# Channel mixing by quarters: seven products in place of eight, on one core

## Chip, cores, metric

One Trainium2 chip (trn2), one of its cores. The metric is the device time of the whole kernel in microseconds (us).

## The reference, cut to what matters

Attention with normalised queries and keys, then an MLP mixer on its output. Everything is fp32 except the four mixer weights, which arrive as 64-bit floats.

```python
# q, k, v: (8, 12, 448, 64)
scores = scale * rmsnorm(q, g_q) @ rmsnorm(k, g_k).transpose(0, 1, 3, 2)
x = softmax(scores) @ v            # then (B, H, S, D) -> (B, S, H*D) = (8, 448, 768)
h = relu(x^T @ w_tok1) @ w_tok2    # token mixing:   448 -> 256 -> 448
u = x + h^T
h2 = relu(u @ w_ch1) @ w_ch2       # channel mixing: 768 -> 1536 -> 768
return u + h2
```

Channel mixing is the larger part: per batch 2 x 72 products of 128x128 weights with 448 columns.

## The kernel before

The eight batches form a pipeline: while TensorE does the MLP of batch b, the attention of batch b+1 is merged between its products. All weights stay in SBUF as fp32. They are made from 64-bit words in 80 chunks of 128x256 (72 for the channel layers), at the start: some beside batch 0's attention, the rest beside batch 0's MLP.

```python
def convert_first(i):     # VectorE: exponent and mantissa bits of the high word
    nc.vector.tensor_scalar(e, hi, 0x7FF00000, None, ALU.bitwise_and)
    nc.vector.tensor_scalar(m, hi, 0x000FFFFF, None, ALU.bitwise_and)
def convert_second(i):    # ScalarE: both as floats
    nc.scalar.activation(out=e, in_=e, func=AF.Relu, bias=expo_c, scale=8.0)
    nc.scalar.activation(out=mf, in_=m, func=AF.Identity, bias=one_c, scale=2.0**-20)
def convert_last(i):      # VectorE: low word and sign; GpSimd: the product
    nc.vector.scalar_tensor_tensor(out=mf, in0=lo, scalar=2.0**-52, in1=mf, op0=ALU.mult, op1=ALU.add)
    nc.vector.scalar_tensor_tensor(out=e, in0=hi, scalar=0x80000000, in1=e,
                                   op0=ALU.bitwise_and, op1=ALU.bitwise_or)
    nc.gpsimd.tensor_tensor(out=dst, in0=fold(mf), in1=fold(ef), op=ALU.mult)

def weight_items(lo, hi):
    def one(i):           # one weight step: three chunks in flight, a load two ahead
        ... convert_first(i); convert_second(i - 1); convert_last(i - 2); weight_load(i + 2)

def ch1(b, f, part):      # 6 products of 448 columns, relu by ScalarE
    for cc in range(part * half, part * half + half):
        nc.tensor.matmul(out=ps[:, 0:S], lhsT=wc1_sb[:, cc, f * P:(f + 1) * P],
                         rhs=st["uT", b][:, cc, :], start=(cc == 0), stop=(cc == NC - 1))
    if part == 1:
        nc.scalar.activation(out=st["h2"][:, f, :], in_=ps[:, 0:S], func=AF.Relu)

def ch2(b, cc, part):     # 12 products of 448 columns, added to u by VectorE
    ...
# order: merge() interleaves lists by their estimated cost
early = merge(early, weight_items(BEFORE, len(chunks) + 2))     # batch 0 only
for _, fn in merge(att, early + late): fn()
```

The order in which `merge` emits the instructions is their order in each engine's queue, so it sets what stands behind what (the stretch from 241 us below shows VectorE standing 4.6 us at one instruction with others behind it).

## Time and profile before

| | before |
|---|---|
| time, median (4 runs) | 1544.6 us (1543.6 to 1547.2) |
| TensorE busy | 1489.2 us, 96% |
| batch 0's MLP | 84 to 288 us |
| a full later batch | 186.7 us |

The start times come from the first transpose of each batch's MLP. In all lines of the profile PE is TensorE's products, PEld its weight loads, DVE VectorE, ACT ScalarE, POOL GpSimd, and SPq the SyncE queue that issues the loads and stores; L181 is line 181 of that run's kernel.

### The profile page before, as it was taken

What the parts mean: (1) busy time and instruction counts of PE and PEld (TensorE: products, weight loads), DVE (VectorE), ACT (ScalarE), POOL (GpSimd) and SP (SyncE); (2) the same over time, 40 slices, a digit from 0 to 9 for tenths busy, and PEclk for the clock granted to TensorE, in tenths of its full rate; (3) what the DMA queues carried; (4) which work ended last, traced back from release to release, by engine and by line L of the source; (5) the groups of instructions that cost most, each with busy time, mean ns of one, the idle gap of its engine ahead of it and who ended that gap; (6) DMA issues with size and microseconds to landing.
All of it is one profiled execution on the core that took longest, in us unless ns stands there. A gap on an engine that the chain in (4) does not pass through costs nothing.

```text
span 1543.7 us, 13746 instructions
## 1 busy us (share of the span) xinstructions
PE 1489.2 (96%) x5248; PEld 715.6 (46%) x5248; DVE 470.8 (30%) x831; ACT 489.9 (32%) x890; POOL 369.7 (24%) x234
## 2 busy tenths in 40 slices
PE   5879999999999999999999999999999999999998
PEld 2334444544444444454445444444444444445554
DVE  5977777231222212231222221223112222112000
ACT  5855655322223232233222323222322323111100
POOL 6755555121212113111221122112211212000000
PEclk9999999999999999999999999999999999999999
DMA  5434443101011010111001100020001100000001
GB/s 122 127 95 120 123 134 113 36 19 30 24 36 37 18 30 24 36 36 30 24 18 36 48 24 18 19 66 24 18 18 36 54 18 7 7 19 18 0 6 31
DMA packets 121742, 65.73 MB, mean 43 GB/s; under 512 B 91780, under 2 KB 111748, under 8 KB 121668
## 3 DMA queue, kind: packets, MB, share of 16 engines
q1 hardware_dynamic: 111138, 53.53, 13.4%
q10 hardware_dynamic: 10530, 11.24, 2.5%
q8 instruction: 43, 0.70, 0.2%
q14 instruction: 31, 0.25, 0.0%
HBM read 53.74 MB, written 11.01 MB: 42 GB/s over the span
## 4 chain that ended last, share of the span: by engine, by line
PE 88%; DVE 4%; DMA 2%; ACT 2%; POOL 1%; issue 1%; SPq 0%; ACTq 0%; DVEq 0%; POOLq 0%
PE m_ps L417 28%; PE m_ps L430 26%; PE s_ps L236 10%; PE o_ps L293 9%; PE m_ps L393 5%; PE m_ps L401 4%; PE m_ps L307 2%; PE t_ps L221 2%; PE t_ps L374 2%; DMA raw<-in_moe_w_ch_dram 1%; POOL rs L572 1%; ACT qkT L223 1%; DVE e_t L148 1%; DVE m_t L149 1%; DVE es L283 1%
## 5 line engine op out<-in xcount | busy, mean ns | idle before, releaser
L430 PE MATMUL m_ps<-h,wc_sb 128*128 128x448 f32 x1152 | 450.4, 542 | 1.5 <-DVE dt L319 1.5
L417 PE MATMUL m_ps<-uT,wc_sb 128*128 128x448 f32 x1152 | 447.8, 543 | 0.0
L417 PEld LDWEIGHTS m_ps<-uT,wc_sb 128*128 128x128 f32 x1152 | 214.3, 190 | 215.7 <-issue 204.9
L430 PEld LDWEIGHTS m_ps<-h,wc_sb 128*128 128x128 f32 x1152 | 212.6, 190 | 207.5 <-issue 206.1
L242 ACT ACTIVATE e<-s_ps,rs 112x448 f32<-112x448 f32 x384 | 212.2, 635 | 185.6 <-PE s_ps L236 184.0
L279 POOL TENSOR_TENSOR es<-e 112x896 f32<-112x896 f32 x48 | 100.1, 2085 | 677.2 <-PE m_ps L307 564.3
L572 POOL TENSOR_TENSOR rs<-ms,mhalf_c 112x16 f32<-112x16 f32 (+1 forms) x49 | 146.0, 2981 | 219.7 <-DVE ms L571 219.0
L236 PE MATMUL s_ps<-qkT 64*112 64x448 f32 x768 | 171.7, 567 | 9.4 <-ACT qkT L223 9.4
L293 PE MATMUL o_ps<-e,vt 112*64 112x448 f32 x768 | 165.5, 552 | 0.0
L421 ACT ACTIVATE h<-m_ps 128x448 f32<-128x448 f32 x96 | 52.2, 544 | 351.0 <-PE m_ps L417 351.0
L319 DVE STREAM_TRANSPOSE dt<-m_ps 128x448 f32<-128x448 f32 x48 | 31.2, 650 | 403.7 <-PE m_ps L307 403.6
L283 DVE TENSOR_TENSOR es<-es,e 112x896 f32<-112x896 f32 x96 | 112.5, 1172 | 76.4 <-ACT e L242 71.7
L435 DVE TENSOR_TENSOR uT<-uT,m_ps 128x448 f32<-128x448 f32 x48 | 29.8, 620 | 330.5 <-PE m_ps L430 330.4
L223 ACT ACTIVATE qkT<-t_ps,g_t 128x448 f32<-128x448 f32 x96 | 58.8, 632 | 206.6 <-PE t_ps L221 206.3
L236 PEld LDWEIGHTS s_ps<-qkT 64*112 64x112 f32 x768 | 62.1, 174 | 107.6 <-issue 87.6
L393 PE MATMUL m_ps<-x,w_sb 112*128 112x384 f32 x256 | 91.1, 506 | 19.4 <-ACT x L379 11.2
L293 PEld LDWEIGHTS o_ps<-e,vt 112*64 112x64 f32 x768 | 46.6, 136 | 108.8 <-issue 108.8
L567 DVE TENSOR_REDUCE ms<-sq 112x16 f32<-112x1024 f32 (+1 forms) x49 | 58.5, 1195 | 117.4 <-ACT sq L564 117.4
L181 POOL TENSOR_TENSOR wc_sb<-m_t,e_t 128x256 f32<-128x256 f32 x72 | 61.8, 866 | 87.0 <-DVE e_t L179 85.4
L401 PE MATMUL m_ps<-w_sb,h 128*128 128x448 f32 x192 | 78.1, 552 | 2.5 <-DVE uT L406 2.5
L379 ACT COPY y<-t_ps 112x512 f32<-112x512 f32 x48 | 28.0, 585 | 156.6 <-PE t_ps L374 156.6
L393 PEld LDWEIGHTS m_ps<-x,w_sb 112*128 112x128 f32 x256 | 47.8, 194 | 57.0 <-ACT x L379 16.6
(43 smaller groups left out, 775.2 us busy)
## 6 DMA issues: line engine op xcount, KB each, us to landing
raw<-in_moe_w_ch_dram SPq DMA_DIRECT2D x72, 256.0 KB, 2.7
vt<-in_v_dram SPq DMA_DIRECT2D x48, 224.0 KB, 2.6
qk<-in_q_dram SPq DMA_DIRECT2D x92, 112.0 KB, 2.8
qk<-in_k_dram SPq DMA_DIRECT2D x92, 112.0 KB, 3.0
out_dram<-y ACTq DMA_DIRECT2D x14, 672.0 KB, 4.4
out_dram<-y ACTq DMA_DIRECT2D x6, 224.0 KB, 2.9
raw<-in_moe_w_tok_dram SPq DMA_DIRECT2D x4, 224.0 KB, 4.6
raw<-in_moe_w_tok_dram SPq DMA_DIRECT2D x2, 256.0 KB, 2.8
```

The costliest lines, as they stand in the source:

```text
L181: nc.gpsimd.tensor_tensor(out=dst, in0=fold(mf), in1=fold(ef), op=ALU.mult)
L223: nc.scalar.mul(st["qkT", p][:, i, :], ps[:, 0:S], g_t[:, i:i + 1])
L236: nc.tensor.matmul(out=ps[0:R, 0:S], lhsT=qkT[a * D:(a + 1) * D, 1, kc * R:(kc + 1) * R], rhs=qkT[a * D:(a + 1) * D, 0, :], start=True, st ...
L242: nc.scalar.activation(out=e[0:R, a, i, :], in_=pss[a][0:R, 0:S], func=AF.Exp, scale=st["rs", p][0:R, r:r + 1])
L279: nc.gpsimd.tensor_tensor(out=es[0:R], in0=e[0:R, :, 0, :], in1=e[0:R, :, 1, :], op=ALU.add)
L283: nc.vector.tensor_tensor(out=es[0:R], in0=es[0:R], in1=e[0:R, :, i, :], op=ALU.add)
L293: nc.tensor.matmul(out=o[a * D:(a + 1) * D, 0:S], lhsT=vt[0:R, a, kc * D:(kc + 1) * D], rhs=e[0:R, a, i, :], start=(kc == 0), stop=(kc == ...
L393: nc.tensor.matmul(out=ps[:, 0:HC], lhsT=w1_sb[0:R, c, jc * P:(jc + 1) * P], rhs=st["x", h][0:R, c, :], start=(c == 0), stop=(c == NS - 1))
L401: nc.tensor.matmul(out=ps[:, 0:S], lhsT=st["h1", jc][:, cc * P:(cc + 1) * P], rhs=w2_sb[:, jc].rearrange("p c r -> p (c r)"), start=(jc == ...
L417: nc.tensor.matmul(out=ps[:, 0:S], lhsT=wc1_sb[:, cc, f * P:(f + 1) * P], rhs=st["uT", b][:, cc, :], start=(cc == 0), stop=(cc == NC - 1))
L430: nc.tensor.matmul(out=ps[:, 0:S], lhsT=wc2_sb[:, f, cc * P:(cc + 1) * P], rhs=st["h2"][:, f, :], start=(f == 0), stop=(f == NF - 1))
L572: nc.gpsimd.tensor_tensor(out=rs[0:R, w], in0=ms[0:R, w], in1=self.mhalf_c[0:R].to_broadcast([R, (hi - lo) * n]), op=ALU.pow)
```

## The change

Both channel layers are cut into quarters (half of the contraction by half of the outputs; the 448 columns into two times 224), and each 2x2 block product is done with seven products in place of eight, in the form that needs few sums (Winograd's form of Strassen's). This needs four sums or differences of the weights' quarters, four of the moving quarters, and a chain of sums of the products. The intent: 1/8 of the channel arithmetic off TensorE. The eight weight blocks (four quarters, four sums) don't fit into SBUF, so they are written to a DRAM buffer once, and each batch streams them back in 42 units of 384 KB, with seven unit buffers.

```diff
-    wc1_sb = const.tile([P, NC, DC], F32, name="wc1_sb")
+    ws1 = dram.tile([KF // 2, NQ, P, KC, 2, P], F32, name="ws1")      # ws2, ws3 likewise
-    ps_O = pool("ps_O", 2, space=PSUM)
-    ps_M = pool("ps_M", 2, space=PSUM)
+    ps_O = pool("ps_O", 1, space=PSUM)
+    ps_M = pool("ps_M", 3, space=PSUM)
...
+    def combine(j):               # after each pair of chunks
+        w, group, m, t = stages[j]
+        q = st.pop("stage")
+        nc.vector.tensor_tensor(out=q[:, 4], in0=q[:, 1], in1=q[:, 3], op=ALU.add)
+        nc.vector.tensor_tensor(out=q[:, 6], in0=q[:, 1], in1=q[:, 0], op=ALU.subtract)
+        nc.gpsimd.tensor_tensor(out=q[:, 5], in0=q[:, 4], in1=q[:, 0], op=ALU.subtract)
+        nc.gpsimd.tensor_tensor(out=q[:, 7], in0=q[:, 2], in1=q[:, 5], op=ALU.subtract)
...
+        nc.sync.dma_start(out=to.rearrange("q p n -> p q n"), in_=q[:])
...
+        at = i - len(first)       # at the end of convert_last(i)
+        if at >= 0 and at % 2 == 1:
+            combine(at // 2)
...
+    PRODUCTS = ((0, "B11"), (2, "B21"), (5, "T2"), (6, "T3"), (4, "T1"), (7, "B22"), (3, "T4"))
...
+    def ch1(b, mp, i):            # product i of 7: 2 x 3 matmuls of 224 columns
+        for j in range(2):
+            for t in range(KC):
+                nc.tensor.matmul(out=ps[:, j * HS:(j + 1) * HS], lhsT=w[:, t, j, :], rhs=m,
+                                 start=(t == 0), stop=(t == KC - 1))
...
+        elif i == 4:              # the sums of products, some by GpSimd
+            nc.scalar.copy(out=r[5], in_=got)
+            add(nc.gpsimd, h("B22"), r[5], r[3])
+            add(nc.gpsimd, r[2], r[2], r[5])
+        elif i == 5:
+            add(nc.vector, r[1], got, r[2])
...
-            early = merge(early, weight_items(BEFORE, len(chunks) + 2))
+            then = len(first) + 2 * stage_end[3] + 2
+            early = merge(early, weight_items(BEFORE, then))
+            late = merge(late[:14], weight_items(then, len(chunks) + 2)) + late[14:]
```

Cuts are marked by "...". Attention and token mixing are as before, but for the accumulators above and the output tiles.

## The prediction

> **What bounds the kernel now.** I read the page first: the busy row, the slices and the chain of the end.
>
> ```profile
> PE 1489.2 (96%) x5248; PEld 715.6 (46%) x5248; DVE 470.8 (30%) x831; ACT 489.9 (32%) x890; POOL 369.7 (24%) x234
> ...
> PE   5879999999999999999999999999999999999998
> ...
> DVE  5977777231222212231222221223112222112000
> ...
> POOL 6755555121212113111221122112211212000000
> ...
> L430 PE MATMUL m_ps<-h,wc_sb 128*128 128x448 f32 x1152 | 450.4, 542 | 1.5 <-DVE dt L319 1.5
> L417 PE MATMUL m_ps<-uT,wc_sb 128*128 128x448 f32 x1152 | 447.8, 543 | 0.0
> ```
>
> TensorE is the bound in nearly all of the span, and the two channel products (L417, L430) are 898 of its 1489 us. The other engines are a quarter to a third busy on the mean, but not at the start: in the first seven slices (270 us) VectorE shows 5 to 9 tenths and GpSimd 5 to 7. That is where the weights are converted from 64-bit words (80 chunks, the last at 268 us). So there are two stages, and I read them apart, in the table of busy times by stretch (PE, PEld, DVE, ACT, POOL):
>
> ```profile
> 20.00:84.00 64.00, 55.65 (x290) 21.82 (x288) 57.18 (x103) 54.57 (x104) 52.00 (x34) 1.00 0.45 113
> 84.00:130.00 46.00, 35.23 (x124) 17.68 (x122) 33.01 (x73) 21.53 (x46) 23.78 (x19) 0.90 0.37 103
> 130.00:270.00 140.00, 136.53 (x464) 63.33 (x464) 101.60 (x255) 80.57 (x168) 75.04 (x67) 1.00 0.43 121
> 507.00:694.00 187.00, 185.39 (x659) 89.03 (x658) 44.95 (x64) 52.89 (x91) 37.01 (x18) 1.00 0.12 30
> ```
>
> The last row is one steady batch: 1.6 us of idle TensorE in 187. Before 84 us (attention of batch 0 alone, with the first weights) VectorE is 89% busy. Batch 0's MLP runs from 84 to 288 us, where the next batch's first transpose starts (from the start times of the transposes in the trace). Each later full batch takes 186.7 us (start times 474.8, 661.5, 848.2).
>
> How fast is a matmul? Weight loads in the timeline, where nothing else stands between:
>
> ```profile
> 801.13 0.19 PEld L430 LDWEIGHTS m_ps<-h,wc_sb 128*128 128x128 f32 x1 [0.19 <-issue]
> 801.50 0.19 PEld L430 LDWEIGHTS m_ps<-h,wc_sb 128*128 128x128 f32 x1 [0.19 <-issue]
> ```
>
> Every fp32 product is two instructions, and one starts each 0.3755 us for 448 columns.
>
> And why are VectorE's 30 to 70% dear at the start? Two rows:
>
> ```profile
> 109.06 2.13 POOL L279 TENSOR_TENSOR es<-e 112x896 f32<-112x896 f32 x1
> ...
> 109.18 2.17 DVE L149 TENSOR_SCALAR m_t<-raw 128x256 uint32<-128x256 uint32 x1
> ```
>
> A VectorE instruction that usually takes 0.28 us stood for 2.17, until GpSimd's was over.
>
> **What the Trainium skill says.** (1) "TensorE: Matmul & The Clock Gate", section "Back-to-back issue gap": columns / 2.4 + 2.5 ns, but in a stream of load-and-multiply pairs 81 ns at 128 columns where the formula has 56. The trace agrees with the formula at 448 columns taken twice per column (2 x 448 / 2.4 + 2.5 = 375.8); for the transposes' 128 columns it has 109 ns, again 2 x 128 / 2.4 + 2.5, so no penalty for loads there. (2) "SBUF — State Buffer", section "Who interferes with whom": a VectorE instruction with two SBUF inputs, or in a 2-port mode, and a GpSimd one that reads SBUF exclude one another for the whole instruction. The two rows above agree; during GpSimd's pow (2.9 us at 113.5) VectorE's weight work ran on at its usual 0.28 to 0.42 us, so pow doesn't do it here. (3) "DMA: Bandwidth & Descriptors", section "Anatomy of one DMA": about 2.0 us plus bytes at 436 GB/s (fitted there to another issuing path). A 256 KB weight chunk lands in 2.7 us here; the formula has 2.6.
>
> **The change, part by part.**
>
> *Removed on TensorE.* Per batch the two channel layers are 2 x 72 products of 448 columns: 288 instructions x 0.3758 = 108.2 us. Now each is 7 quarter products: 3 x 7 x 2 x 3 = 126 in the first, 7 x (2 + 1) x 6 = 126 in the second, of 224 columns: 504 instructions x (2 x 224 / 2.4 + 2.5 = 189.2 ns, an estimate) = 95.3 us. **Gain 12.9 us a batch, 103 us in all**; the 1/8 less arithmetic loses 0.6 us to the fixed 2.5 ns. A 128-column weight load is shown at 190 ns, starting with the matmul before it; but a transpose starts 24 ns before its load's shown end, so the load just hides. This is the closest call.
>
> *Added, steady batches.* VectorE: per 448-column pass 0.62 us (L435's row): 21 in layer 1 (13 us), 14 in layer 2 (half of them 224 wide, 7 us), six small differences (2 us), less the 6 old adds (3.7): 45 becomes 64 us. GpSimd: twelve 448-wide at about 1.1 us (from 2085 ns for 896), four more and ten of 224: 37 becomes 65. ScalarE: 53 becomes 61. In a batch of 174 us none is near a bound. The chain product 4 - ScalarE copy - two GpSimd adds - VectorE add takes some 3.8 us against 2.3 us of one product, and three accumulators give two products of slack; a GpSimd burst (sum, pow, scale: 7 us a head pair) can use that up now and then. I choose **+1.5 us a batch, 10 us in all**.
>
> *Moved to DMA.* 42 units of 393 KB a batch, 132 MB in all, 16.5 MB in 174 us or 95 GB/s, where the start already moves 121. A unit lands in about 2.9 us (estimate by point 3), and it is asked for six units, some 13 us, ahead. Hidden after batch 0.
>
> *Added, batch 0.* Here is the price. The 72 big chunks are converted as before, and each pair of chunks gets two VectorE and two GpSimd sums of 128x128 (about 0.2 and 0.42 us, scaled from 0.34 and 0.73 for 256) and a store. Both layers' sums must be out and back before use. I count the time in which VectorE or GpSimd (pow left out) has an instruction open, since they mostly exclude each other: in the trace 60.6 of the 64 us up to 84, and 127 of 140 from 130 to 270. A steady batch has 50, of which 41 attention; so the 54 chunks from 130 to 270 cost (127 - 0.685 x 41 - 5) / 54 = 1.74 us each.
> - Stage 1 takes 23 weight steps in place of 16: 7 x 1.74 + 6 sums x 1.24 = 20 us: ends at 104 in place of 84.
> - Batch 0's token mixing and layer 1 carry 47 chunks: 82 us, their sums 29, 65% of a batch's attention 27, the MLP's own VectorE work 21 and the part of its GpSimd work that can't overlap, some 12: 171 us, against TensorE's 70 + 34 = 104. **So VectorE and GpSimd become the bound of this stage**; at 98% use it ends near 278. I choose 275 (some PSUM reads overlap).
> - The first unit of layer 2 waits for the last store and its own load: two DMAs of about 3 us and GpSimd's work, 8 us.
> - Layer 2, 12 weight steps beside it in its first part: 48; again a store and a load, 4 visible; the last third 25.
> Batch 0 ends at 275 + 8 + 48 + 4 + 25 = 360; before, 288: **72 us lost**, 59 of it if I allow for a better overlap than in the stretches measured. I choose 63.
>
> Sum: 1545 - 7 x 12.9 (batches 1 to 7) + 10 + 63 = 1528; batch 0's gain is inside its 63. I shade to **1525 us**.
>
> **The rivals.** (a) The preparation is hidden after all: from 130 to 270 us TensorE was 97% busy beside it, so there may be more room than the open-instruction count shows (a blocked instruction counts as open). Then batch 0 loses 20 us and the time is about 1485. (b) Half-width products don't run at 189 ns: if the load shows by 11 ns, 504 x 8 x 0.011 = 44 us more, about 1570. For it: the skill's 81 ns; against: 109 ns in the transposes. (c) The in-order queues bite in steady batches: ScalarE's relu waits for GpSimd, the exps stand behind it. At 5 us a batch: 1550. (d) The unit loads bind: 95 GB/s against up to 216 seen for moments at the start speaks against it.
>
> **Range and chances.** 1485 to 1560: rival (a) is the low end, (b) or (c) in part the high end. Faster by 2% means under 1514.4: batch 0 has to lose 52 us or less with the steady gain whole, 38%. Slower by 2% (over 1576) needs (b) or (c) in full with my batch 0: 4%. The rest, 58%, is within 2%.
>
> **What would show it.** The quarter products' weight loads 0.189 us apart; later batches about 175 us long; VectorE and GpSimd at 8 to 9 tenths up to some 270 us, and TensorE at 6 to 7 tenths there; a gap of 6 to 10 us before layer 2 of batch 0, ended by a DMA; the second batch's first transpose at about 350. Wrong if that transpose starts before 320 (preparation cheaper) or a batch takes over 180 (products or queues dearer).

## More of the kernel before

The prediction shows the main lines of the page. Here are three more: the granted TensorE clock in tenths over 40 slices of the span, the share of the DMA engines' time, and the loads of the weight chunks (count, size, us to landing).

```profile
PEclk9999999999999999999999999999999999999999
DMA  5434443101011010111001100020001100000001
...
raw<-in_moe_w_ch_dram SPq DMA_DIRECT2D x72, 256.0 KB, 2.7
```

The clock is at 90% or more in every slice, the DMA engines are half busy while the weights come in and nearly idle after. So TensorE is the bound, and a change that takes arithmetic from it seems right.

## The result

The kernel after takes 1571.3 us (median of 4, 1569.4 to 1573.3), before 1544.6: the ratio is **1.017** (95% interval 1.0151 to 1.0189). A ratio is the mean time of one kernel's fast runs over that of the other's of the same rounds, so not quite the ratio of the medians. The change made the kernel slower by 1.7%: inside 2%, but outside the range of 1485 to 1560. Results are correct.

The page of the kernel after: busy row, five rows of slices (tenths in 40 slices of the span), and the group of one channel layer.

```profile
PE 1422.2 (90%) x6976; PEld 1054.9 (67%) x6976; DVE 662.5 (42%) x1183; ACT 511.1 (33%) x930; POOL 612.6 (39%) x514
...
PE   5765866497999999999999999999999999999997
...
DVE  5765866743344233432434234433343225322321
...
POOL 5674566644235324333235224352334234320231
PEclk9786997798999999999999999999999999999999
DMA  5456667476244552455244542555254433444353
...
L581 PE MATMUL m_ps<-hb,unit 128*128 128x224 f32 x2016 | 402.0, 357 | 31.4 <-DMA unit<-ws 31.4
```

TensorE has 67 us less of busy time, and the span is 28 us longer. From the 11th slice on it is full as before. In the first ten slices (393 us) it is at 4 to 9 tenths, its clock is no longer full, and yet VectorE shows only 3 to 8 tenths and GpSimd 4 to 7. The table by stretch has the columns of the prediction (busy us and count of PE, PEld, DVE, ACT, POOL, then clock, DMA share, GB/s). The stretches are batch 0's attention, its token mixing, its layer 1, its layer 2, and one steady batch:

```profile
20.00:112.00 92.00, 67.58 (x283) 24.85 (x280) 68.28 (x136) 58.66 (x113) 62.38 (x50) 0.85 0.45 122
112.00:185.00 73.00, 45.85 (x151) 21.57 (x150) 47.26 (x112) 28.66 (x60) 39.52 (x45) 0.77 0.61 179
185.00:292.00 107.00, 80.87 (x361) 60.58 (x360) 75.51 (x177) 46.90 (x96) 65.03 (x71) 0.87 0.68 205
292.00:400.00 108.00, 73.07 (x367) 59.63 (x366) 53.56 (x114) 30.55 (x61) 49.56 (x55) 0.84 0.63 191
574.90:749.40 174.50, 172.41 (x875) 129.50 (x874) 65.33 (x98) 55.27 (x97) 63.04 (x44) 1.00 0.44 127
```

The last row is the steady gain as predicted: a batch takes 174.5 us, before 186.7. So the two traces differ in two ways:

| | before | predicted | after |
|---|---|---|---|
| attention of batch 0 ends | 84 | 104 | 112.5 |
| batch 0's layer 1 ends | | 275 | 292 |
| batch 0's layer 2 really starts | | 283 | 318 |
| batch 1's MLP starts | 288 | 360 (63 lost, so 351, in the sum) | 400 |
| from there to the end | 1255.5 | 1175 | 1171 |

From batch 1 on the kernel gains 84 us; up to there it loses 112.

### The profile page after: what moved, and what is told of

Same layout as the page of the kernel before. It is cut to its first block, busy times and chain, and to the rows that moved or that the text cites. A ratio compares the mean times of both kernels' runs of the same rounds, so it can differ in the third digit from the quotient of the medians.

```text
span 1571.7 us, 19052 instructions
## 1 busy us (share of the span) xinstructions
PE 1422.2 (90%) x6976; PEld 1054.9 (67%) x6976; DVE 662.5 (42%) x1183; ACT 511.1 (33%) x930; POOL 612.6 (39%) x514
## 4 chain that ended last, share of the span: by engine, by line
PE 76%; DVE 8%; POOL 6%; DMA 3%; issue 3%; ACT 2%; ACTq 1%; SPq 0%; POOLq 0%; DVEq 0%
PE m_ps L581 24%; PE m_ps L523 22%; PE s_ps L289 8%; PE o_ps L346 8%; PE m_ps L445 5%; PE m_ps L453 4%; PE d_ps L360 2%; POOL rs L754 2%; DMA raw<-in_moe_w_ch_dram 2%; POOL stage L231 2%; PE t_ps L424 2%; PE t_ps L274 2%; DVE m_t L202 1%; DVE m_t L227 1%; DVE e_t L229 1%
## 5 line engine op out<-in xcount | busy, mean ns | idle before, releaser
L581 PE MATMUL m_ps<-hb,unit 128*128 128x224 f32 x2016 | 402.0, 357 | 31.4 <-DMA unit<-ws 31.4
L581 PEld LDWEIGHTS m_ps<-hb,unit 128*128 128x128 f32 x2016 | 378.5, 192 | 53.7 <-issue 26.5
L523 PE MATMUL m_ps<-tu,unit 128*128 128x224 f32 x1152 | 232.9, 356 | 4.3 <-DVE r L528 4.3
L523 PEld LDWEIGHTS m_ps<-tu,unit 128*128 128x128 f32 x1152 | 217.6, 192 | 14.8 <-issue 8.5
L754 POOL TENSOR_TENSOR rs<-ms,mhalf_c 112x16 f32<-112x16 f32 (+1 forms) x49 | 148.6, 3033 | 103.2 <-DVE ms L753 94.3
L523 PE MATMUL m_ps<-uT,unit 128*128 128x224 f32 x864 | 179.4, 360 | 3.3 <-DVE r L528 3.3
L523 PEld LDWEIGHTS m_ps<-uT,unit 128*128 128x128 f32 x864 | 163.5, 193 | 22.6 <-issue 13.7
L590 POOL TENSOR_TENSOR uT<-uT,r 128x448 f32<-128x448 f32 (+1 forms) x64 | 58.7, 928 | 283.9 <-DVE r L590 168.0
L590 DVE TENSOR_TENSOR uT<-uT,m_ps 128x448 f32<-128x448 f32 (+1 forms) x80 | 38.8, 502 | 195.3 <-PE m_ps L581 160.5
L528 DVE TENSOR_TENSOR r<-m_ps,r 128x448 f32<-128x448 f32 x72 | 44.9, 623 | 137.8 <-PE m_ps L523 94.1
L231 POOL TENSOR_TENSOR stage<-m_t,e_t 128x256 f32<-128x256 f32 x72 | 56.0, 779 | 101.2 <-DVE e_t L229 99.0
```

The costliest lines, as they stand in the source:

```text
L523: nc.tensor.matmul(out=ps[:, j * HS:(j + 1) * HS], lhsT=w[:, t, j, :], rhs=m, start=(t == 0), stop=(t == KC - 1))
L528: add = lambda e, o, x, y: e.tensor_tensor(out=o, in0=x, in1=y, op=ALU.add)
L581: nc.tensor.matmul(out=ps[:, j * HS:(j + 1) * HS], lhsT=st["w"](j, t), rhs=hb[:, HB[what], t, :], start=(t == 0), stop=(t == KF - 1))
L590: add = lambda e, o, x, y: e.tensor_tensor(out=o, in0=x, in1=y, op=ALU.add)
L754: nc.gpsimd.tensor_tensor(out=rs[0:R, w], in0=ms[0:R, w], in1=self.mhalf_c[0:R].to_broadcast([R, (hi - lo) * n]), op=ALU.pow)
```

## The experiments

Every run but the last two is one time and a profile (its state is unknown, as for any single run on one core); the kernel before gave 1545.4 to 1546.9 us in the same calls, so differences of 5 us are safe. "Theory A" below is that VectorE stands in its queue for GpSimd; "B" that the work of VectorE and GpSimd, which exclude one another, fills the stage (the prediction's); "C" that the weight loads stand behind the stores; "D" that TensorE's clock and its waits hold the stage.

What suggests A is this stretch of the kernel after (start us, us, engine, line; in brackets the idle time before and what ended it):

```profile
241.69 3.75 POOL L754 TENSOR_TENSOR rs<-ms,mhalf_c 112x16 f32<-112x16 f32 x1
245.51 1.04 POOL L265 TENSOR_TENSOR qk<-qk,rs 112x512 f32<-112x512 f32 x1
246.51 0.72 POOL L231 TENSOR_TENSOR stage<-m_t,e_t 128x256 f32<-128x256 f32 x1
...
247.27 0.29 DVE L178 TENSOR_TENSOR stage<-stage 128x128 f32<-128x128 f32 x1 [4.60 <-POOL stage L231]
```

The pow (L754, the power -1/2 of a norm's mean square) and the scaling of the next heads hold GpSimd's queue; the product of the chunk (L231) comes after them, and VectorE, whose next instruction is the chunk's first sum (L178), idles 4.6 us. In the kernel before, VectorE stood for this product (L181 there) 12.9 us in 7 waits. The sum of such waits from 20 to 400 us is shown with the first experiment.

### Sums one weight step later (e1_late_sums)

```diff
-            combine(at // 2)                       # in convert_last
+            pending.append((at // 2, st.pop("stage")))
         def one(i):
             ... convert_first(i); convert_second(i - 1)
+            combine_pending()
             ... convert_last(i - 2); weight_load(i + 2)
```

> The sums and the store of a pair of weight chunks are emitted one weight step later, so that VectorE has other work between its last conversion and the first sum. Theory A (VectorE stands in its in-order queue for GpSimd's product: 66 us in 36 waits, up to 5.7 us each behind GpSimd's pow): these waits go to under 20 us, batch 1's first transpose moves from 400 to 345-370 us, the time is 1515-1545. Theory B, my prediction's (VectorE and GpSimd exclude each other and are full): no more than 8 us saved, 1563 or more. Theory C (the weight loads stand behind the stores on the SyncE queue): little, since the store still stands ahead of the next load; 1555-1571.

Measured: 1573.9 us, nothing gained. The waits, kernel after and then this run (who waited for whom: us in total, times, longest):

```profile
DVE stage L178 <- POOL stage L231: 66.0, 36, 5.7
```

```profile
DVE e_t L200 <- DMA raw<-in_moe_w_ch_dram: 40.0, 22, 4.3
...
DVE stage L177 <- POOL stage L230: 25.9, 12, 4.6
```

```profile
SPq L187 <- DVE stage L178: 85.8, 35, 6.8
```

VectorE's wait for GpSimd fell from 66.0 to 25.9 us, and 40.0 us of waiting for raw chunks took its place, where the kernel after had 8.7. The last row is the SyncE queue of this run: the store stands there for the now later sums, and the next chunk's load is behind it.

### Loads ahead of the stores (e2_load_first)

```diff
-            combine(at // 2)
+            pending.append((at // 2, st.pop("stage")))
             ... convert_last(i - 2); weight_load(i + 2)
+            combine_pending()                      # same step, behind the load
```

> Only the order on the SyncE queue changes: in each weight step the next chunk's load is issued before the sums' store, not behind it. The order on VectorE and GpSimd is as in the kernel after. Theory C: the loads no longer wait for the sums, VectorE's waits for the raw chunks shrink, batch 1 starts 20-40 us earlier, 1530-1550. Theory A: VectorE still stands for GpSimd's product, less than 15 us saved. Theory B: less than 8 us saved.

Measured: 1569.7 us, 2 us less. Theory C alone falls too.

### Without the sums (e3_no_sums)

```diff
-        nc.vector.tensor_tensor(out=q[:, 4], ...); nc.vector.tensor_tensor(out=q[:, 6], ...)
-        nc.gpsimd.tensor_tensor(out=q[:, 5], ...); nc.gpsimd.tensor_tensor(out=q[:, 7], ...)
-        nc.sync.dma_start(out=to..., in_=q[:])
+        for half in range(2):                      # quarters stored twice
+            nc.sync.dma_start(out=to[4 * half:4 * half + 4]..., in_=q[:, 0:4])
```

> Wrong results on purpose: the four sums of each pair of chunks are left out, and the four plain quarters are stored twice, so the stored bytes and the loads stay. Theory B: the sums' own time goes, 36 x 1.24 = 45 us of VectorE and GpSimd, some 35-45 us saved, 1526-1536. Theory A: the sums' time and VectorE's 66 us of waiting for GpSimd go, 50-80 us saved, 1490-1520. Theory C: the store waits for one GpSimd instruction less chain, 15-30 us saved.

Measured: 1546.3 us. Its output is wrong, which doesn't matter for the time. 25 us saved, under what B and A expected, in the range of C, which e2 had refuted. The sums are not the bulk of the loss. (The waits of A and C stay in this run, and as e5_both shows they can hide a saving, so 25 us is what the sums cost in this order.)

### Without the preparation (e4_no_prep)

```diff
-            convert_first / convert_second / convert_last / weight_load of the 72 channel chunks
+            combine((i - 2 - n1) // 2)             # only the 36 stores, of a constant tile
```

> Wrong results on purpose: the 72 channel weight chunks are neither loaded nor converted nor summed; a constant tile is stored in their place, 36 stores as before. This measures what all of the preparation costs. If the quarter products themselves cost nothing beyond their TensorE time, batch 1's first transpose comes at about 70 + 174 = 245 us and the time is 1410-1430 (the seven later batches as in the kernel after, 1171 us). If the first use of the stored sums by itself costs a wait (store and load back to back), it shows here as a gap before a channel product of 4-8 us. A time over 1450 would mean that something other than the preparation holds batch 0 back.

Measured: 1435.9 us. Its output is wrong, which doesn't matter for the time. Batch 1's MLP starts at 264 us in place of 400, and the page of this run has TensorE full from the fourth slice:

```profile
PE 1384.7 (97%) x6976; PEld 1040.2 (73%) x6976; DVE 533.9 (37%) x823; ACT 451.4 (31%) x786; POOL 514.4 (36%) x371
...
PE   5889999999999999999999999999999999999998
```

So loading, converting and summing the channel weights costs **135 us** in the kernel after. (A part of it the kernel before pays as well; how much was not measured.) The time is 6 us over the 1410 to 1430 expected, and batch 1's MLP comes 19 us later than the 245 us expected: the attention of batch 0 ended at 90 us, where about 70 had been taken. From there its MLP took 173.5 us, as long as a steady batch, and no gap of 2 us stands before a channel product; so nothing else of the change holds batch 0's MLP back.

The stretch up to batch 1's MLP, in the kernel after and then in this run (columns as above):

```profile
0.00:400.20 400.20, 273.41 (x1174) 170.09 (x1175) 249.26 (x553) 171.51 (x337) 223.22 (x231) 0.85 0.60 176
```

```profile
0.00:263.80 263.80, 235.88 (x1174) 155.31 (x1175) 118.12 (x193) 111.02 (x193) 124.53 (x88) 0.99 0.69 195
```

TensorE has the same 1174 instructions in both, in 273 us of busy time there and 236 here. So of the 136 us between the two, 37 are products that took longer, at a granted clock of 0.85 against 0.99, and 99 are idle TensorE. That sizes the clock's part in D.

### Both orders together (e5_both)

```diff
-    raw_pool = pool("raw_pool", 4); y_pool = pool("y_pool", 3)
+    raw_pool = pool("raw_pool", 5); y_pool = pool("y_pool", 2)
             ... convert_first(i); convert_second(i - 1); convert_last(i - 2)
-            weight_load(i + 2)
+            weight_load(i + 3)
+            if i % 2 == 0 or i == hi - 1:
+                combine_pending()                  # a step later, and behind the load
```

> The two changes that did nothing alone, together, and one load more in flight: the sums come a whole weight step after the conversion, the loads go out ahead of the stores, and a fifth raw buffer lets them go three chunks ahead (the output tiles go from 3 to 2 buffers to make room). Theory A+C (two waits in series, each hiding the other: in the run with late sums VectorE waited 40 us for raw chunks in place of 66 us for GpSimd): both waits go, the pace of the chunks falls from 4.1 to under 3.5 us, 1530-1550. Theory B (the work of VectorE and GpSimd, which exclude each other, was 173 us of the 203 of the stage in my count and 92% with pow, so there is nothing to win by order): 1560 or more.

Measured: 1553.5 us, 18 us saved where each half alone had saved 2 or nothing. From 180 to 285 us VectorE and GpSimd have gone up to 86% and 74%:

```profile
180.00:285.00 105.00, 75.54 (x350) 55.87 (x348) 90.49 (x195) 49.63 (x103) 77.20 (x84) 0.88 0.73 220
```

Counting from the trace's records the time in which VectorE or GpSimd has an instruction open: in the kernel after 173 us of the 203 from 112 to 315 us without pow, 187 with it (92%); in this run 166 of the 190 from 110 to 300 us, 177 with pow (93%). In layer 1 alone the count with pow is 95% in the kernel after (185 to 292 us) and over 99% here (180 to 285 us). So A and C together cost 18 us, and each hides the other; that B stands behind them is what the count suggests and the lighter conversion tests. (The fifth raw buffer and the third load ahead came with the two orders and were not tried by themselves, so a part of the 18 us may be theirs.)

### A lighter conversion (e6_int, and e7_before_int for the kernel before)

The exponent of a 64-bit float becomes that of a 32-bit one by leaving out three bits (for the sizes that weights have), so three exact bit operations do the work of seven instructions, truncating where the old form rounds:

```diff
-    2 x tensor_scalar (VectorE), 2 x activation (ScalarE),
-    2 x scalar_tensor_tensor (VectorE), 1 x tensor_tensor (GpSimd)
+    nc.vector.tensor_scalar(a, hi, 3, 0x3FFFFFFF, ALU.logical_shift_left, ALU.bitwise_and)
+    nc.vector.scalar_tensor_tensor(out=a, in0=hi, scalar=0xC0000000, in1=a,
+                                   op0=ALU.bitwise_and, op1=ALU.bitwise_or)
+    nc.vector.scalar_tensor_tensor(out=dst.bitcast(U32), in0=fold(lo), scalar=29, in1=fold(a),
+                                   op0=ALU.logical_shift_right, op1=ALU.bitwise_or)
```

> The order stays as in the kernel after, but the work shrinks: a 64-bit word becomes a float by three bit operations on VectorE (no ScalarE, no GpSimd product) in place of four on VectorE, two on ScalarE and one on GpSimd. By the durations in the trace a chunk then costs about 0.9 us of VectorE alone in place of 1.74 of VectorE and GpSimd. Theory B: 72 x 0.84 = 60 us less work at 85 to 92% use, 1500-1510, and the stage is still bound by both. Theory A (VectorE's wait for GpSimd's product is what costs): that wait is gone as well, 1480-1510; this run doesn't tell A from B, it tells both from theory D: what holds the stage is TensorE's own clock, 0.77 to 0.87 there, and waits between TensorE and the rest, in which case less than 25 us are saved, 1546 or more.

Measured: 1500.4 us, correct. **71 us saved** with the order of the kernel after: as A and B expected, and D, which expected under 25, falls as the main cause. The run doesn't tell work from order: with GpSimd's product gone, VectorE no longer waits for it, and a chunk is first read two weight steps later, so that its load has more time. What the lighter work is worth in the better order is told by e8_int_order against e5_both (68 us) and e12_best against e11_order_early (63 us).

> The kernel before with the same three bit operations for the conversion, for a fair comparison with the run above. There the weights' stage was nearly hidden (TensorE 97% busy from 130 to 270 us); idle TensorE before 130 us is some 27 us, of which 13 are the first loads. So 10-20 us saved at most: 1525-1537.

Measured: 1532.9 us, correct: 13 us saved. The same lighter work is worth five times as much in the kernel after, because there the preparation is what ends the stage.

### The lighter conversion in the better order (e8_int_order), ended earlier (e9_int_early), moved ahead (e10_int_more)

The handover is the place where TensorE takes over the last prepared weights: last sum, store, load back, first product.

```diff
 e8:  raw_pool 6, weight_load(i + 4), combine_pending() as in e5; in a step the third operation of
      chunk i - 2, the second of i - 1, the first of i
 e9:  as e8, and
-            early = merge(early, weight_items(BEFORE, then))
-            late = merge(late[:14], weight_items(then, len(chunks) + 2)) + late[14:]
+            early = merge(early[:-4], weight_items(BEFORE, then)) + early[-4:]
+            late = merge(late[:10], weight_items(then, len(chunks) + 2)) + late[10:]
 e10: as e9, BEFORE = len(first) + 21 in place of + 15
```

> The bit-operation conversion (1500 us) with the order of the run e5_both: loads four chunks ahead in six buffers and ahead of the stores, the sums a step later, and the three bit operations of a chunk spread over three weight steps, so that none depends on the one just before it (in the run e6_int such a dependent one took 0.43 us and started 0.46 after the other; an independent one starts after 0.34). If the stage is bound by the work of VectorE and GpSimd (B): 72 x 0.25 = 18 us less on VectorE, 1480-1490. If order still matters as well: down to 1470. If TensorE's clock and its waits hold it (D): 1495-1500.

Measured: 1485.6 us.

> As e8_int_order, and the weight steps are ended four TensorE items (9 us) before each of the two places where TensorE waits for a just stored weight: the last four of batch 0's layer 1, the last four of layer 2's first part. The waits for unit loads (22.8 us in e6_int) should fall to under 8, so 8-15 us under e8_int_order if TensorE is what ends the stage; no change if the preparation itself is, since its work stays the same and only ends later in the item order.

Measured: 1468.4 us, 17 us under e8_int_order, a little more than expected.

> As e9_int_early, with six weight steps more in the first stage (29 in place of 23), where VectorE is 88% busy and TensorE 84%. If the sum of work binds, it is only moved: within 4 us of e9_int_early. If batch 0's MLP is where TensorE loses most (its clock is 0.86 to 0.92 there, 1.00 in the first stage), 5-10 us faster.

Measured: 1475.6 us, 7 us slower, which neither theory expected. The first stage became longer (94 in place of 86 us) and layer 1 ended 9 us later; why the moved work is not made up for is open.

### Order and handover alone (e11_order_early), and the best kernel timed (e12_best)

e11 is e5_both with the two lines of e9 above: no work is changed. e12 is e9 again.

> No change of the work: the kernel after with the order of e5_both (1553) and the weight steps ended four TensorE items before each of the two places where TensorE waits for a stored weight, as in e9_int_early, the conversion as it was. If the handover costs what it did in the lighter kernel, 12-18 us less than e5_both: 1535-1542, about the kernel before (same). If the preparation's own work is the end of the stage (B), it still ends when it ends and TensorE waits for it elsewhere: 1548-1554. In no case under 1525, since 173 us of VectorE and GpSimd work remain in the stage.

Measured: 1533.9 us (1532.4 to 1536.5, 4 runs), ratio to before **0.9927** (0.991 to 0.9943): 20 us under e5_both, slightly better than expected for the case that the handover counts. The last sums that layer 2's first part needs went to their store at 282 us, in e5_both at 292: the preparation itself ended 10 us earlier, though its work was the same. So it had been held up by its place among the other items too, and not by its own work alone.

> The kernel of e9_int_early again, timed in three rounds: 1466-1471, faster than the kernel before by 4.7 to 5.2%, with correct results. The kernel before with the same conversion (e7_before_int) was 1533, so about 4.2% are the quarter products and 0.8% the conversion.

Measured: 1470.8 us (1470.2 to 1473.1, 4 runs), ratio to before **0.9522** (0.9506 to 0.9538), correct. The 4.8% include the lighter conversion; against the kernel before with the same conversion (e7_before_int, one time) it is 62 us, 4.0%. TensorE's waits for unit loads at the start, in the kernel after, in e5_both, in e11_order_early and in e12_best (who waited for whom: us in total, times, longest):

```profile
PE m_ps L581 <- DMA unit<-ws: 31.4, 2, 24.9
```

```profile
PE m_ps L589 <- DMA unit<-ws: 32.4, 3, 22.4
```

```profile
PE m_ps L589 <- DMA unit<-ws: 7.1, 3, 4.5
```

```profile
PE m_ps L581 <- DMA unit<-ws: 2.7, 2, 1.6
```

And layer 1 of batch 0 in e12_best, which takes 88 us where it took 107:

```profile
136.00:224.00 88.00, 75.22 (x355) 57.22 (x353) 78.59 (x176) 22.76 (x41) 54.53 (x57) 0.94 0.94 287
```

VectorE is 89% busy in it, and the DMA engines show a share of 0.94 (0.68 in the kernel after): which of the two holds this layer now was not tried. What is left over the 1436 us without preparation is 35 us.

## Why the prediction was wrong

**What held.** The quarter products run at 0.189 us each; here are twelve weight loads of the kernel after in 2.27 us:

```profile
699.82 2.27 PEld L581 LDWEIGHTS m_ps<-hb,unit 128*128 128x128 f32 x12
```

So rival (b) is out. The steady batch was to gain 12.9 us less 1.5 of queueing and gained 12.2: rival (c) is out as well; and with a DMA share of 0.44 in the steady stretch no product waits for a unit there: rival (d) is out. That the preparation would turn the start from TensorE's bound into VectorE's and GpSimd's held in kind (e4, e6), and so rival (a) is out.

**The step that failed: "Added, batch 0", with "at 98% use it ends near 278. I choose 275", and then "72 us lost ... I choose 63".** It was 112. The work in that step was sized well: 171 us counted, 173 us of open VectorE or GpSimd instructions (pow left out) found between 112 and 315 us. (Only the sum was checked, so that it fits so closely may be luck.) What was mis-sized is the use of the two engines: 85%, not 98%, so the preparation ended at 311 to 315 us and not at 278. The 98% was higher than in either stretch that I had counted (60.6 of 64 us is 95%, 127 of 140 is 91%). Two things stand behind the low use, and their shares overlap:
- Order, 18 us (e5_both against after). VectorE waits in its queue for GpSimd's product, and the loads on the SyncE queue stand behind stores that wait for both. I named neither for batch 0. The two lie on one loop (load, convert, sum, store, next load), and the mending of one alone showed nothing (e1, e2).
- Pow. I left it out since it doesn't block VectorE's instructions. It does hold GpSimd's queue, and VectorE waits for what is behind it. With pow counted the use is 92%.

**The second step: "two DMAs of about 3 us and GpSimd's work, 8 us".** TensorE waited 24.9. The chain that ended last, round that wait (start us, us, what):

```profile
310.80 0.59 POOL stage L181
...
311.41 3.19 DMA ws<-stage
...
314.75 3.46 DMA unit<-ws
...
318.25 2.61 PE m_ps L581 x6
```

The two DMAs are 6.7 us, as I had said. But TensorE had come to this place at 293, and the last sum was done at 311: the 18 us between are the preparation's lag. The prediction took for granted that TensorE would be late as well, since it set one time for both. Ending the weight steps four items before the end of each part of TensorE's work takes 20 us off (e11 against e5): it then has other work in its queue, and the preparation itself ends earlier. So this is mostly the lateness of the first step, seen from TensorE, and not a second sum to add to it.

**The shading and the signs.** The sum gave 72 us; I went down to 63, on the ground that an instruction that is blocked counts as open. The error went the other way. The first stage, too, took 29 us more than before where I had 20. And my signs of being wrong asked for a cheaper preparation or for dearer products; a dearer preparation, which came, had no sign and no rival.

**What stays open.** TensorE's clock (0.77 to 0.87 of full speed in the stretches of the first 400 us; before, 0.90 from 84 to 130 us and 1.00 in the other stretches) was not changed by itself. By e4 the longer products are 37 of the 136 us, and they shrink when only the other engines' work does: TensorE's busy time in all is 1422.2 us in the kernel after, 1396.6 in e12, 1384.7 in e4. So the clock is a part of the loss, not its main cause. The steps from after over e5, e11 and e12 down to e4 add up to the 135 us by construction (18, 20, 63 and 35 left), but each share depends on what was mended before it (the lighter conversion gave 71 us as the first step, 63 as the last), e12 also has one raw buffer and one load ahead more than e11, and the 25 us of the sums overlap with all of them.

## What to carry to other kernels

Arithmetic that is taken from the bound engine in every batch is paid for in preparation on engines that looked a third busy on the mean: read their load in the stage in which the preparation runs, and with a use well under full (here 85%) for engines that wait for one another. A wait that is mended alone can come back as another in the same loop; before a theory of order is dropped, mend all the waits of the loop together. And let the last preparation end some TensorE items before its first use: the store and the load back (6.7 us) and the lag of the slower engine are then behind other work.

## What the Trainium skill lacked or had wrong

- "SBUF — State Buffer", section "Who interferes with whom": the exclusion for the whole instruction agrees with L149 (2.17 us beside GpSimd's 2.13 us sum, else 0.28). It has no exception for a GpSimd instruction that reads little: pow on 112x16, whose two inputs lie in SBUF, took 2.9 us, and VectorE's weight instructions ran beside it at 0.28 to 0.42 us.
- "TensorE: Matmul & The Clock Gate", section "Back-to-back issue gap": it gives about 81 ns a product at 128 columns in a stream of loads and products, over its own formula. Here products of 224 columns, each with its own load, start 189 ns apart, which is 2 x 224 / 2.4 + 2.5: no time for the loads shows. In "Part 1: The HAM clock gate" the page also has the clock fall to half after an idle window of some 3.4 us. The trace agrees, nearly: in the first 400 us the clock is granted at half in 17 stretches, and each begins within 5 us of the start of a TensorE gap of 2.9 to 24.9 us (one gap more, of 3.3 us, is followed by none); before, a gap of 2.4 us went ahead of one. The steady batch, whose gaps are under 1.5 us, has 1.00.
- "DMA: Bandwidth & Descriptors", section "Anatomy of one DMA": 2.0 us plus bytes at 436 GB/s gives 2.9 us for a 384 KB unit and 3.2 for a 512 KB store. Measured medians, on another issuing path than the page's fit: 3.3 and 3.5; and 4.3 for the units in the first 400 us, where the DMA share is 0.45 to 0.68. In e12's layer 1, at a share of 0.94, it is 6.4 for a unit and 5.7 for a store. The page's formula has no term for such load.
- No page that I used tells of two waits in series hiding one another (VectorE's 66.0 + 8.7 us of waiting for GpSimd and for loads became 25.9 + 40.0, and the time stayed).
